# A recurrent attention layer and two MoE-shaped layers on one core: states in 64 columns, other start order, decay bounds in layer 2

## The chip, the core and the metric

The kernel runs on 1 core of one Trainium2 chip. The metric is the device time of one execution in microseconds (us). Most work is done by five engines that each run their own list of instructions in order: TensorE (PE in the profile; PEld is its loading of weights), VectorE (DVE), ScalarE (ACT), GpSimd (POOL) and SyncE (SP), which here only issues DMA transfers. Semaphores tie the lists together.

## The reference

The first part is a recurrent attention over 768 steps for 4 batches and 8 heads of 48 columns; its output goes through two feed-forward layers with 3072 tokens, 384 model columns and 2048 hidden ones.

```python
for t in range(S):
    cur = einsum('bhd,bhe->bhde', u[None] * kt, vt)
    y[:, :, t] = einsum('bhd,bhde->bhe', rt, state + cur)
    state = wt[:, :, :, None] * state + einsum('bhd,bhe->bhde', kt, vt)
x = y.transpose(0, 2, 1, 3).reshape(B * S, H * D)
h = x @ w_in;  x = (maximum(h, 0) + alpha * minimum(h, 0)) @ w_out      # layer 1
h = x @ w_in;  x = (h * clip(h + 3, 0, 6) / 6) @ w_out                  # layer 2
```

## The kernel before

**Attention.** The 768 steps are cut into thirds of 256 (12 in all, counted over the batches as t), and the 8 heads into 4 pairs. A unit n is one third of one pair; there are 48, and each third is two chunks (c) of 128 steps. The two heads of a pair lie on partitions 0 to 47 and 64 to 111. For a unit, L673 loads keys, reads and decays in one transfer; L691 and L705 are VectorE scans that give the products of decays to a chunk's end and their inverses; L726 scales keys and reads by them (`scale`); L781 multiplies scaled keys with reads for each head (48 rows, 128 columns, one PSUM bank per head); L789 transposes the keys, L820 copies them out; L827 and L831 make key-value products for the two heads; L876 or L878 brings the state Y to the next chunk. `state` (L853 on ScalarE, L855 on VectorE) scales Y into the tile sbd, a 112x112 matrix that is zero outside the two 48x48 diagonal blocks, with one instruction for each block. L764 puts the u terms on diagonals of X, L805 or L810 copies the triangle of L781's product over them. `pc` then sums the output y in PSUM: L907 multiplies sbd with the scaled reads (112 rows to 112 columns at once), L914 and L918 add X times v for the two heads (128 rows to 48 or 64 columns). Each fp32 product is two instructions in the trace. L702 (`keep`) keeps the smallest products of each unit for a check at the end.

**From attention to layer 1.** L943 and L949 split y into a high part and a rest (`hi_`, `lo_`), and write them into xt, the input of layer 1 for one block of 512 tokens (two thirds). Pairs 0 to 2 fill 112 of the 128 rows of their slab; the rows of pair 3 go to a tile x3, and six transfers per third (`spread`, L959) distribute 16 rows each to the free rows of the three slabs. They follow all eight outputs of the third.

**Layers.** A slot is one group of 128 hidden columns of one block: nine matmuls into h (L1176 to L1178: high by high, high by rest, rest by high, for three slabs), a gate on ScalarE and VectorE (L1214 and L1221, L1216 and L1225, L1231, L1234), and nine matmuls into three sums acc. There are 16 slots in a block, 6 blocks and 2 layers. The weights arrive packed; L128, L132, L135, L1140 and L1144 unpack them and split them likewise.

**Order.** Nothing of the order is left to a tool: class `Plan` collects all steps, each with the engines that may do it, an estimated duration for each, a due time and what it depends on. `run` then builds the lists greedily: the engine that can start earliest takes the step with the earliest due time. The tables URGENCY, GROUPS and SINGLE shift due times and fix engines. `issue` stands for SP, where a later transfer lands after an earlier one. Before the first slot, `keep_warm` fills gaps of TensorE with small matmuls (L1036), for the clock that is granted to it.

**Where.** Units 0 to 7 (`early`) feed block 0 and come before the first slot. Units 0 to 15 have TensorE steps of their own; later ones join the outputs of one unit with the key-value products of the next (`add_visit`) and the next unit's L781. In layer 2 the weights and the decays of units 24 to 47 are checked for range (`add_range`, `add_decay`), with slack.

Of the kernel before, what the change touches and what calls it, by code (L numbers as in the profile page):

```python
# [7 lines left out]
F32 = mybir.dt.float32  # L8
# [33 lines left out]
WARM = 400  # L42
SETTLE = 3
FUSE = 16
# [97 lines left out]
def weight_range(nc, v, raw):  # L142
# [8 lines left out]
    "add_drain.drain": {2: (-2.0, "DVE"), 3: (2.0, "ACT")},  # L151
    "add_drain.store": {2: (-6.75, None), 3: (-0.25, None)},
    "add_range.upper": {4: (2.5, None)},
    "add_slot.gate": {1: (-4.5, None), 2: (-3.0, None), 3: (-2.25, None)},
    "add_slot.ghi": {1: (-4.25, None), 2: (-5.0, None), 3: (-10.75, None)},
    "add_slot.glo": {1: (-1.5, "DVE"), 2: (3.75, None), 3: (-3.75, None)},
    "add_slot.h_": {1: (4.0, None), 2: (-4.0, None), 3: (-6.75, None), 4: (-1.0, None)},
    "add_slot.pq": {1: (-6.5, None), 2: (1.25, None), 3: (1.25, None)},
    "add_third.load_rk": {0: (1.25, None), 1: (-6.0, None), 2: (-2.25, None), 3: (-3.75, None)},
    "add_third.load_v": {0: (-4.5, None), 1: (-0.5, None), 2: (1.25, None), 3: (-5.75, None)},  # L160
    "add_third.red": {0: (-2.0, None), 1: (-4.25, None), 2: (7.0, None), 3: (-7.0, None)},
    "add_unit.add_output.hi_": {0: (-3.5, None), 1: (-6.75, None), 2: (3.25, None), 3: (-8.75, None)},
    "add_unit.add_output.lo_": {0: (-0.5, None), 1: (-2.75, None), 2: (-6.5, None), 3: (5.25, None)},
    "add_unit.add_states.newstate": {0: (-14.25, None), 1: (-4.5, None), 2: (-1.0, None), 3: (6.0, None)},
    "add_unit.check": {2: (-5.5, None), 3: (-7.25, None)},
    "add_unit.diag": {0: (-5.25, None), 1: (3.25, None), 2: (-5.25, None), 3: (-9.75, None)},
    "add_unit.keep": {0: (-0.25, None), 1: (4.75, None), 2: (-3.25, None), 3: (-18.0, None)},
    "add_unit.kt": {0: (-8.75, None), 1: (0.75, None), 2: (-6.5, None), 3: (-3.25, None)},
    "add_unit.kv": {0: (-4.5, None)},
    "add_unit.load": {0: (-3.25, None), 1: (-6.75, None), 2: (-5.75, None), 3: (3.75, None)},  # L170
    "add_unit.pa": {0: (-8.25, None), 1: (-2.75, None)},
    "add_unit.recip": {0: (-0.25, None), 1: (-3.25, None), 2: (8.5, None)},
    "add_unit.scan_g": {0: (-2.5, None), 1: (-5.5, None), 2: (-5.0, None), 3: (8.25, None)},
    "add_unit.scan_t": {0: (5.75, None), 1: (-9.75, None), 2: (6.75, None), 3: (-12.5, None)},
    "add_unit.triangle": {0: (-2.0, None), 1: (-4.0, None), 2: (2.25, None), 3: (-1.5, None)},
    "add_weights.hi": {0: (3.0, None), 1: (1.25, None)},
    "add_weights.lo": {0: (3.5, "POOL"), 1: (-2.25, None)},
    "add_weights.load": {0: (-3.75, None), 1: (-2.0, None)},
    "add_weights.rest": {0: (17.25, None), 1: (-1.75, None)},
    "join": {0: (-1.5, None), 1: (0.25, None)},  # L180
    "load_alpha": {0: (-5.75, None)},
    "load_u": {0: (-3.5, None)},
    "negate": {0: (-7.5, None)},
    "output": {0: (-4.5, None), 1: (-5.75, None)},
    "scale": {0: (0.5, None), 1: (-2.25, None), 2: (-0.5, None), 3: (-2.0, "DVE")},
    "scale_half": {0: (-5.0, "POOL")},
    "second": {1: (-2.25, None), 2: (-5.25, None), 3: (5.5, None), 4: (2.0, None)},
    "sign": {0: (3.0, None), 1: (5.25, None)},
# [153 lines left out]
class Plan:  # L342
# [165 lines left out]
    def keep_warm(self, seq):  # L508
# [3 lines left out]
        for o in seq:  # L512
            if o.get("filler"):
                continue
# [1106 lines left out]
```

## Time and profile before

| what | us |
|---|---|
| median of 3 runs | 928.58 |
| lowest and highest run | 927.21, 931.37 |
| the profiled execution | 926.92 |
| its span from the first to the last instruction | 925.1 |
| TensorE busy in the span | 912.8 |
| VectorE busy | 551.1 |
| ScalarE busy | 520.8 |
| GpSimd busy | 121.9 |

Busy time of TensorE counts from an instruction's start to its modelled end, and instructions overlap: a 512-column matmul is shown with 0.39 us, while the next one starts 0.23 us behind it. The step from start to start is what counts in a full string. An idle time stands in brackets with what ended it.

### The profile page before, as it was taken

How to read it: one execution, taken by the hardware profiler on the slowest of the kernel's cores; microseconds unless marked ns; L12 is line 12 of the kernel's file. 1: busy time of each engine (PE TensorE's matmuls, PEld its weight loads, DVE VectorE, ACT ScalarE, POOL GpSimd, SP SyncE). 2: the span in 40 equal slices, each digit the busy share in tenths (PEclk: the TensorE clock that was granted, in tenths of full speed). 3: DMA queues.
4: the chain of work that ended last, by engine and by line, in shares of the span. 5: the costliest groups of instructions: out<-in, count | busy, mean ns of one | idle time of the engine just before them, and what ended most of it. 6: DMA issues, size and time to landing. Idle time of an engine off the chain costs nothing.

```text
span 925.1 us, 13568 instructions
## 1 busy us (share of the span) xinstructions
PE 912.8 (99%) x4936; PEld 749.0 (81%) x4936; DVE 551.1 (60%) x1061; ACT 520.8 (56%) x1174; POOL 121.9 (13%) x109
## 2 busy tenths in 40 slices
PE   8889999999999999999999999999999999999998
PEld 6677788888888888888888888888888888888886
DVE  8989988667878655753347775343353443443432
ACT  5989974545545545453359997363363453553332
POOL 4410120011021231311022241000000000000000
PEclk9999999999999999999999999999999999999999
DMA  9888333222323302110136530060250330430001
GB/s 279 259 260 278 99 89 99 72 60 84 114 68 99 112 17 70 31 44 10 35 119 214 192 124 1 24 203 9 75 161 1 113 122 1 119 118 1 35 1 38
DMA packets 39628, 88.97 MB, mean 96 GB/s; under 512 B 5248, under 2 KB 10368, under 8 KB 39552
## 3 DMA queue, kind: packets, MB, share of 16 engines
q1 hardware_dynamic: 39120, 87.22, 30.7%
q8 instruction: 41, 0.67, 0.3%
q10 hardware_dynamic: 432, 0.79, 0.2%
q14 instruction: 35, 0.29, 0.1%
HBM read 76.19 MB, written 9.44 MB: 93 GB/s over the span
## 4 chain that ended last, share of the span: by engine, by line
PE 94%; DVE 3%; DMA 2%; SPq 0%; issue 0%; ACT 0%; DVEq 0%
PE h L1176 14%; PE acc L1176 14%; PE h L1177 14%; PE h L1178 14%; PE acc L1177 14%; PE acc L1178 14%; PE A L781 3%; PE y L914 2%; PE y L907 2%; PE A L789 1%; DMA wraw<-in_w 1%; DMA un<-in_unit 1%; PE y L918 0%; DVE tg L691 0%; DVE rk L635 0%
## 5 line engine op out<-in xcount | busy, mean ns | idle before, releaser
L1176 PE MATMUL acc<-g,w 128*128 128x512 f32 x576 | 226.6, 393 | 0.0
L1177 PE MATMUL acc<-g,w 128*128 128x512 f32 x576 | 224.3, 389 | 0.0
L1178 PE MATMUL acc<-g,w 128*128 128x512 f32 x576 | 224.3, 389 | 0.0
L1231 ACT ACTIVATE g<-pg 128x512 fp32r<-128x512 f32 x192 | 120.6, 628 | 126.3 <-PE acc L1178 106.5
L1234 DVE TENSOR_TENSOR g<-pg,g 128x512 fp32r<-128x512 f32 x141 | 99.9, 709 | 132.8 <-ACT g L1231 132.5
L1176 PEld LDWEIGHTS acc<-g,w 128*128 128x128 f32 x576 | 108.6, 189 | 22.7 <-issue 0.6
L1178 PEld LDWEIGHTS acc<-g,w 128*128 128x128 f32 x576 | 108.1, 188 | 22.6
L1177 PEld LDWEIGHTS acc<-g,w 128*128 128x128 f32 x576 | 108.2, 188 | 21.8 <-DVE g L1234 0.3
L1225 DVE SCALAR_TENSOR_TENSOR pg<-q,h 128x512 f32<-128x512 f32 x96 | 65.7, 685 | 95.2 <-ACT q L1216 95.0
L1234 POOL TENSOR_TENSOR g<-pg,g 128x512 fp32r<-128x512 f32 x51 | 73.6, 1444 | 363.6 <-ACT g L1231 250.6
L1216 ACT ACTIVATE q<-h,three 128x512 f32<-128x512 f32 x96 | 65.8, 685 | 92.6 <-PE h L1178 92.5
L1176 PE MATMUL h<-xt,w 128*128 128x512 f32 x288 | 115.0, 399 | 2.0 <-DMA xt<-x 2.0
L1178 PE MATMUL h<-xt,w 128*128 128x512 f32 x288 | 112.7, 391 | 0.0
L1177 PE MATMUL h<-xt,w 128*128 128x512 f32 x288 | 112.6, 391 | 0.0
L1176 PE MATMUL h<-x,w 128*128 128x512 f32 x288 | 112.0, 389 | 0.0
L1177 PE MATMUL h<-x,w 128*128 128x512 f32 x288 | 112.0, 389 | 0.0
L1178 PE MATMUL h<-x,w 128*128 128x512 f32 x288 | 112.0, 389 | 0.0
L1214 ACT ACTIVATE q<-h,nal 128x512 f32<-128x512 f32 x96 | 65.7, 685 | 82.2 <-PE h L1178 77.8
L1221 DVE SCALAR_TENSOR_TENSOR pg<-h,q 128x512 f32<-128x512 f32 x96 | 65.9, 686 | 40.0 <-ACT q L1214 25.2
L764 ACT ACTIVATE X<-ident,p 128x128 f32<-128x128 f32 x192 | 60.6, 390 | 11.7 <-PE y L918 11.3
L1176 PEld LDWEIGHTS h<-xt,w 128*128 128x128 f32 x288 | 54.8, 190 | 13.4 <-DMA xt<-x 2.1
L1178 PEld LDWEIGHTS h<-xt,w 128*128 128x128 f32 x288 | 54.3, 189 | 11.5
(102 smaller groups left out, 1222.4 us busy)
## 6 DMA issues: line engine op xcount, KB each, us to landing
wraw<-in_w SPq DMA_DIRECT2D x64, 384.0 KB, 5.6
un<-in_unit SPq DMA_DIRECT2D x48, 337.3 KB, 3.5
raw<-in_w SPq DMA_DIRECT2D x32, 384.0 KB, 3.3
rk<-in_tok SPq DMA_DIRECT2D x24, 384.0 KB, 3.8
v<-in_vch SPq DMA_DIRECT2D x12, 384.0 KB, 4.1
x2d<-st SPq DMA_DIRECT2D x18, 256.0 KB, 2.2
x2r<-x2d SPq DMA_DIRECT2D x18, 256.0 KB, 5.0
out<-st SPq DMA_DIRECT2D x15, 256.0 KB, 2.6
```

The lines of the kernel that those rows point to most:

```text
L764: nc.scalar.activation(X[:, i], ident, AF.Copy, scale=pp[:, i : i + 1])
L781: nc.tensor.matmul(A[h][:, cs], kr[r0 : r0 + D, 0, cs], kr[r0 : r0 + D, 1, cs], start=True, stop=True,)
L907: nc.tensor.matmul(y[:, cs], S[c], u["kr"][:, 1, cs], start=(c == inter[0]), stop=False, skip_group_check=True,)
L1176: nc.tensor.matmul(ps, whi, xhi, start=start, stop=False, skip_group_check=True)
L1177: nc.tensor.matmul(ps, whi, xlo, start=False, stop=False, skip_group_check=True)
L1178: nc.tensor.matmul(ps, wlo, xhi, start=False, stop=stop, skip_group_check=True)
L1214: nc.scalar.activation(q, k["h"], AF.Relu, scale=nal[:, f : f + 1])
L1216: nc.scalar.activation(q, k["h"], AF.Relu, bias=three)
L1221: nc.vector.scalar_tensor_tensor(out=p, in0=k["h"], scalar=0.0, in1=k["q"], op0=ALU.max, op1=ALU.subtract)
L1225: nc.vector.scalar_tensor_tensor(out=p, in0=k["q"], scalar=6.0, in1=k["h"], op0=ALU.min, op1=ALU.mult)
L1231: nc.scalar.activation(k["g"][:, 0], k["p"], AF.Copy)
L1234: eng[e].tensor_tensor(out=k["g"][:, 1], in0=k["p"], in1=k["g"][:, 0].bitcast(F32), op=ALU.subtract)
```

## The change

- `sbd` has 64 columns instead of 112, and both heads' states lie in its columns 0 to 47, on their own rows. `state` scales them in one instruction of 112x48. `pc` multiplies each head apart: rows 0 to 47 into y rows 0 to 63, rows 64 to 111 into y rows 64 to 111.
- The pairs of a third run in the order 3, 0, 1, 2. After each of pairs 0, 1 and 2, two transfers spread the rows of x3 that this pair's slab needs, with high part and rest in one. For units 3 and 7 (`SPLIT`) output is written in two row halves, and their transfers wait for pair 3 alone.
- Units 0 to 3 (`PARTED`) load their decays first and keys and reads in a second transfer.
- The outputs y of odd units below 8 use a bank of the pool of h.
- `keep` is done for units 24 to 47 only; for units 0 to 23 `add_decay` repeats the scan in layer 2 and copies the smallest products.
- The matmuls that fill TensorE before the first slot are no longer a fixed supply, and the rule for the gaps that they leave has changed. ScalarE instead of GpSimd fills `wa`.
- The planner has other constants, and the three tables other values (not shown).

```diff
-WARM = 400
+PARTED = 4
+SPLIT = (3, 7)
...
-    LOAD = 1.3
+    LOAD = 1.25
+    FIRST, RUSH, SLUGGISH = 2.7, 12.0, 1.2
...
-    COLD = 8.0
+    COLD = 0.0
...
-    SLACK, STARTED, STEADY = 0.5, 5.0, 15.0
-    BEGIN = {"PE": 1.5, "DVE": 4.0, "ACT": 6.0, "POOL": 4.0, "SP": 0.7}
+    SLACK, IDLE, SPAN, STARTED = 0.45, 0.7, 3.4, 5.0
+    BEGIN = {"PE": 1.5, "DVE": 2.8, "ACT": 4.3, "POOL": 2.6, "SP": 0.7}
...
+            if o["eng"] == "PE" and not began:
+                gap = o["start"] - t
+                idle = [(a, x) for a, x in idle if a > o["start"] - self.SPAN]
+                slack = max(0.0, min(self.SLACK, gap, self.IDLE - sum(x for a, x in idle)))
...
-    sbd = [const.tile([PR, PR], F32, name=f"sbd{i}") for i in range(4)]
+    sbd = [const.tile([PR, 64], F32, name=f"sbd{i}") for i in range(4)]
...
-            nc.gpsimd.memset(wa[i], 0)
+            nc.scalar.activation(wa[i], none.broadcast_to([P, 2 * DM]), AF.Copy)
...
-        t, pr = divmod(n, NPAIR)
+        t, pr = n // NPAIR, (n + 3) % NPAIR
...
-        o_load = plan.op({"SP": 0.95}, d - 4 if n else -50.0, load, new=[ub_])
+        at = d - 4 if n else -50.0
+        if n < PARTED:
+            o_load = plan.op(
+                {"SP": 0.35}, at - 0.2, lambda e: load(e, 2 * TH, UW), new=[ub_],
+                kind="add_unit.load",
+            )
+            o_in = plan.op(
+                {"SP": 0.63}, at, lambda e: load(e, 0, 2 * TH), new=[ub_], kind="load_kr"
+            )
+        else:
+            o_in = o_load = plan.op({"SP": 0.95}, at, load, new=[ub_])
...
-        plan.op({"ACT": 0.21}, d + 2, keep, [o_t], use=[tgb])
+        if n >= LATER:
+            plan.op({"ACT": 0.21}, d + 2, keep, [o_t], use=[tgb])
...
-            F = u["T"][:, c, 0:1]
-            for r0 in (0, 64):
-                rows, block = slice(r0, r0 + D), S[c][r0 : r0 + D, r0 : r0 + D]
-                if e == "ACT":
-                    nc.scalar.activation(block, Y()[rows, :], AF.Copy, scale=F[rows])
-                else:
-                    nc.vector.tensor_scalar(block, Y()[rows, :], F[rows], None, op0=ALU.mult)
+            F, block = u["T"][:, c, 0:1], S[c][:, 0:D]
+            if e == "ACT":
+                nc.scalar.activation(block, Y(), AF.Copy, scale=F)
+            else:
+                nc.vector.tensor_scalar(block, Y(), F, None, op0=ALU.mult)
...
         def room(e):
+            if alt:
+                return ps_h.tile([PR, 2, TH], F32, tag="h", name=f"y{n}")
             return ps_a.tile([PR, 2, TH], F32, tag="y", name=f"y{n}")
...
-                nc.tensor.matmul(
-                    y[:, cs], S[c], u["kr"][:, 1, cs], start=(c == inter[0]), stop=False,
-                    skip_group_check=True,
-                )
+                for r0, m in ((0, 64), (64, D)):
+                    nc.tensor.matmul(
+                        y[r0 : r0 + m, cs], S[c][r0 : r0 + D, 0:m], u["kr"][r0 : r0 + D, 1, cs],
+                        start=(c == inter[0]), stop=False, skip_group_check=True,
+                    )
...
+            rows = ((0, D), (64, PR)) if split else ((0, PR),)
...
             if pr == 3:
...
+                x3_ops[t] = [o_hi, o_lo]
+                return
...
+            def spread(e, h):
+                nc.sync.dma_start(
+                    XT[j][48 + 64 * h : 64 + 64 * h, pr, :, cs].bitcast(F32),
+                    X3[t][64 * h + 16 * pr : 64 * h + 16 * pr + 16].bitcast(F32),
+                )
+
+            before = x3_ops[t] + ([] if split else [o_hi, o_lo])
+            for h in range(2):
+                ops.append(
+                    plan.op(
+                        {"SP": 0.15}, d + 2.6 - (3.0 if split else 0.0),
+                        lambda e, h=h: spread(e, h), before, new=[xt_buf[j]], use=[x3b_[t]],
+                        kind="spread",
                     )
...
+        for c in range(2):
+            last = [
+                plan.op(
+                    {"DVE": 0.73}, due + 1 + c, lambda e, c=c: falls(e, c), [o] + last, new=[fb],
+                    use=[rb], pair=True, kind="decay_falls",
+                )
+            ]
+            last = [
+                plan.op(
+                    {"DVE": 0.15}, due + 1.5 + c, lambda e, c=c: lowest(e, c), last, use=[fb],
+                    kind="decay_lowest",
+                )
+            ]
```

`falls` is the scan of L691 on one unit's decays (112x258), `lowest` a copy of two values per partition into `fall`.

## Rows read from the trace of the kernel before

**Rows 1.** The page's part 1: busy us (share of the span) and count per engine.

```profile
PE 912.8 (99%) x4936; PEld 749.0 (81%) x4936; DVE 551.1 (60%) x1061; ACT 520.8 (56%) x1174; POOL 121.9 (13%) x109
```

**Rows 2.** Windows: length, PE, PEld, DVE, ACT, POOL busy; clock, DMA share, GB/s.

```profile
50.00:56.00 6.00, 5.25 (x17) 4.30 (x18) 3.81 (x9) 3.45 (x9) 1.09 (x1) 0.72 0.91 286
56.00:130.00 74.00, 74.00 (x452) 58.48 (x451) 69.61 (x131) 68.18 (x141) 10.35 (x9) 1.00 0.61 194
130.00:430.00 300.00, 300.00 (x1889) 248.47 (x1888) 206.73 (x451) 151.94 (x417) 52.77 (x39) 1.00 0.24 69
430.00:905.00 475.00, 475.00 (x2097) 393.15 (x2096) 221.92 (x354) 255.34 (x489) 37.51 (x26) 1.00 0.26 81
```

**Rows 3.** Waits of TensorE over the span: us in total, times, longest us.

```profile
PE A L827 <- ACT kT L820: 2.3, 5, 0.7
PE h L1176 <- DMA xt<-x: 2.0, 1, 2.0
```

**Rows 4.** SP's timeline from 43 us, and the chain that ended last (start, us).

```profile
44.01 4.45 SPq L959 DMA_DIRECT2D xt<-x  x6
...
47.87 2.77 DMA xt<-x
```

**Rows 5.** Timeline of TensorE, 50 to 59 us: start, us, instruction, idle time before.

```profile
50.75 0.77 PE L1176 MATMUL h<-xt,w 128*128 128x512 f32 x1 [2.01 <-DMA xt<-x]
...
56.09 0.39 PE L1178 MATMUL h<-xt,w 128*128 128x512 f32 x1
```

**Rows 6.** Timeline of VectorE, 0 to 54 us.

```profile
8.01 0.70 DVE L691 TENSOR_TENSOR_SCAN tg<-un,restart 112x258 f32<-112x258 f32 x1 [1.92 <-DMA un<-in_unit]
...
39.28 0.43 DVE L949 TENSOR_TENSOR xt<-y,xt 112x256 fp32r<-112x256 f32 x1
...
43.58 0.41 DVE L949 TENSOR_TENSOR x<-y,x 112x256 fp32r<-112x256 f32 x1
```

**Rows 7.** Groups of VectorE, 0 to 44 us: busy us, mean ns, idle before.

```profile
L705 DVE TENSOR_TENSOR_SCAN tg<-un,gfirst 112x258 f32<-112x258 f32 x10 | 7.5, 746 | 0.1
L691 DVE TENSOR_TENSOR_SCAN tg<-un,restart 112x258 f32<-112x258 f32 x10 | 6.7, 681 | 2.3 <-DMA un<-in_unit 2.3
...
L642 DVE TENSOR_REDUCE p<-rk 128x8 f32<-128x384 f32 x6 | 3.3, 544 | 0.1
L635 DVE TENSOR_TENSOR rk<-rk,u_sb 128x384 f32<-128x384 f32 x6 | 3.2, 538 | 0.0
...
L878 DVE SCALAR_TENSOR_TENSOR Y<-Y,tg,A 112x48 f32<-112x48 f32 x12 | 3.0, 252 | 0.0
...
L855 DVE TENSOR_SCALAR sbd<-Y,tg 48x48 f32<-48x48 f32 x6 | 2.6, 431 | 0.0
```

**Rows 8.** The tile x (x3 of the code), 0 to 60 us: its transfers.

```profile
DMA to landing us min/median/max: 2.0/3.4/5.8
```

**Rows 9.** Timeline of TensorE, 60.8 to 63 and 65.1 to 67.4 us.

```profile
61.37 0.72 PE L781 MATMUL A<-kr 48*128 48x128 f32 x8
...
65.37 0.39 PE L1178 MATMUL h<-xt,w 128*128 128x512 f32 x1
65.60 0.60 PE L907 MATMUL y<-kr,sbd 112*112 112x128 f32 x4
66.13 0.31 PE L914 MATMUL y<-X,v 128*48 128x128 f32 x1
66.14 0.31 PE L918 MATMUL y<-X,v 128*48 128x128 f32 x1
66.28 0.27 PE L914 MATMUL y<-X,v 128*48 128x128 f32 x1
```

**Rows 10.** Lines L781 (60 to 75 us) and L914 (65 to 67): min/median/max ns.

```profile
L781 PE MATMUL A<-kr x16: 272/272/373, 61.4 to 69.5; 48*128 48x128 f32 x16
...
L914 PE MATMUL y<-X,v x4: 272/273/310, 66.1 to 66.5; 128*48 128x128 f32 x4
```

**Rows 11.** Groups of TensorE, 56 to 430 us.

```profile
L907 PE MATMUL y<-kr,sbd 112*112 112x128 f32 x132 | 20.8, 272 | 0.0
```

More of the change, by code (lines that the diff above doesn't have):

```diff
@@ L176 @@
[L176 to L185, printed above, removed]
@@ new lines @@
+    "add_weights.hi": {0: (0.25, None), 1: (-2.25, None)},
+    "add_weights.lo": {0: (-6.75, None), 1: (-1.5, None)},
+    "add_weights.load": {1: (-2.5, None)},
+    "add_weights.rest": {0: (3.0, None), 1: (-2.0, None)},
+    "join": {0: (-7.25, None)},
+    "load_alpha": {0: (-2.0, None)},
+    "load_kr": {0: (2.0, None)},
+    "load_u": {0: (-1.0, None)},
+    "negate": {0: (-13.5, None)},
+    "output": {0: (5.25, None), 1: (3.0, None)},
+    "scale": {0: (1.0, "POOL"), 1: (-1.0, "POOL"), 2: (3.0, None), 3: (-3.0, None)},
@@ L416, in step @@
         else:
-            d = o["where"][e] * (2 if e == "PE" and t < self.COLD else 1)
+            d = o["where"][e]
             if e == "PE" and state["began"] and t - state["PE"] > self.LULL:
@@ L947, in lo_ @@
             def lo_(e):
                 hi, lo = parts()
-                nc.vector.tensor_tensor(out=lo, in0=u["y"], in1=hi.bitcast(F32), op=ALU.subtract)
-            fresh = [xt_buf[j]] + ([x3b] if x3b else [])
-            o_hi = plan.op({"ACT": 0.6}, d + 2.5, hi_, [o_pc], new=fresh, use=[yb2])
-            o_lo = plan.op({"DVE": 0.41}, d + 2.5, lo_, [o_hi], new=fresh, use=[yb2])
+                for a, b in rows:
+                    nc.vector.tensor_tensor(
+                        out=lo[a:b], in0=u["y"][a:b], in1=hi[a:b].bitcast(F32), op=ALU.subtract
+                    )
@@ L954, in add_output @@
+            fresh = [xt_buf[j]] + ([x3b_[t]] if pr == 3 else [])
+            more = len(rows)
+            o_hi = plan.op({"ACT": 0.06 + 0.46 * more}, d + 2.5, hi_, [o_pc], new=fresh, use=[yb2])
+            o_lo = plan.op({"DVE": 0.07 + 0.34 * more}, d + 2.5, lo_, [o_hi], new=fresh, use=[yb2])
             ops += [o_hi, o_lo]
             if pr == 3:
[L958 to L962 removed]
@@ L1026, in fast_path, with warm @@
     warm_t = {}
-    def add_warm(count):
-        plan.group = "warm"
-        wb = plan.buf("acc2", 1)
-        def warm(e):
-            if "ps" not in warm_t:
-                warm_t["ps"] = ps_acc.tile([P, 2 * P], F32, tag="acc2", name="warm")
-            some = ident.bitcast(BF16)
-            nc.tensor.matmul(warm_t["ps"], some[:, 0:P], some, start=True, stop=True)
-        for i in range(count):
-            plan.op({"PE": 0.27}, 1000.0, warm, new=[wb])["filler"] = True
+    def warm(e):
+        if "ps" not in warm_t:
+            warm_t["ps"] = ps_acc.tile([P, 2 * P], F32, tag="acc2", name="warm")
+        some = ident.bitcast(BF16)
+        nc.tensor.matmul(warm_t["ps"], some[:, 0:P], some, start=True, stop=True)
+    plan.warm = {
+        "fn": warm, "kind": "add_warm.warm", "filler": True, "id": -1, "due": 1000.0,
+        "group": "warm", "where": {"PE": 0.27}, "full": set(), "order": set(), "pair": False,
+    }
     def add_settle(due, after):
```

292 lines of the change are left out of this document (142 added, 150 removed), and 86 rows, old and new, of the table SINGLE.

## The prediction

> **What bounds the kernel now.** I read the page first: TensorE is busy 99% of the span [rows 1], so time can leave in three ways only: fewer or cheaper matmuls, less time before TensorE is fed without a break, or waits taken out. The table of windows tells which of them is open in which stretch [rows 2]. From 56 to 130 us TensorE is full, but VectorE (69.6 of 74 us) and ScalarE (68.2) are nearly full too. From 130 to 430 us, the rest of layer 1, only TensorE is full; from 430 us on (layer 2) VectorE is below half. The table of TensorE's waits confirms it: the two longest sums are 2.3 us for kT, in five pieces, and 2.0 us in one piece for a transfer into xt before the first slot, which starts at 50.75 us [rows 3, 5]. So the kernel is a start of 50.75 us followed by an unbroken string of matmuls up to 920 us. The change can win in the start, and whatever it adds to TensorE's string it pays in full.
>
> **Where the start ends.** The last output of units 0 to 7 leaves VectorE at 43.58 + 0.41 = 43.99 us [rows 6]. Then SP issues six spread transfers from 44.01 us on, 4.45 us of issuing, and the last of them lands 2.77 us after its issue at 47.87 us [rows 4]. The first slot starts at 50.75 us. Its 18 matmuls reach to 56.09 + 0.23 us, 5.57 us, where 18 steps of the usual 0.227 us (65.60 less 65.37 [rows 9]) are 4.08 us. These 1.5 us are the clock: it was granted at 0.72 of full speed on average in 50 to 56 us, after 2.01 us in which TensorE stood idle [rows 2, 5]. The mean lies between the two levels of 1.2 and 2.4 GHz: the string was entered at the lower one.
>
> **The tail of the start.** After the change the pair of the third that supplies the spread rows comes first, each later pair spreads its own 16 rows by two transfers, and for units 3 and 7 these wait only for the third's first pair. So none of the six issues lies behind unit 7. What is left behind it is its own output, now in two halves: one more VectorE instruction of 0.41 us [rows 6] and one more on ScalarE that I put at as much, together 0.8 us. The gain is 50.75 - 43.99 - 0.8 = 5.9 us. It is smaller if unit 6's two transfers land late: they are issued some 39.28 + 0.43 + 0.6 = 40.3 us, and a spread took 2.0 to 5.8 us to land [rows 6, 8]. At worst 46.1 us, a gain of 4.6 us.
>
> **The start itself.** VectorE works through 10 to 44 us almost without a gap, so work that leaves it, or is put off, counts. Up to 44 us it holds [rows 7]: of six 48x48 state instructions (2.6 us in all) three of 112x48 remain, 0.25 each as L878 takes for that shape, 1.8 us saved; work for units 8 and 9 that the first slot doesn't need, two of the ten L691 (0.68 each), one L705 (0.75), four L635 (0.54) and two L642 (0.54), 5.3 us; and the 1.92 us of idle time before unit 1's scan at 8.01 us, which waited for a load [rows 6] and now needs only that load's last third, with some 0.3 us before unit 0's. Together 9.3 us if the new order uses all of it and nothing else becomes late, 0 if the chain through GpSimd, TensorE and ScalarE, which also took its turns here, is what counts. No row decides between the ends, so I take half, 4.7 us. The first slot then starts at 50.75 - 5.9 - 4.7, some 40.1 us (35.5 to 46.1).
>
> ScalarE loses the L702 copies and the second state instructions, and gets two fills of wa before its first real work; GpSimd loses these fills. Splitting the first four unit loads costs SP four more issues, 0.74 us each by L959's rate (4.45 us for six [rows 4], the dearest at hand), that stand ahead of later loads: 0 as long as VectorE has other work, at most 3.0 us, which the lower end of that gain includes.
>
> **Work that falls back into the string.** TensorE did units 8 and 9 in part while it waited for the first slot. With the slot 10.6 us earlier, about one unit (2.0 us in the string) is still to be done after it; 0 to 3.1 us.
>
> **The clock.** The new padding bounds the idle time before the first slot and the wait for the transfer is gone: -1.5 us (0 at worst).
>
> **What is added to TensorE.** Each L907 product of 112 rows and 112 columns becomes two of 48 rows, one into columns 0 to 63 and one into 64 to 111. The count of L907 doubles. Whether this costs streaming time is read from the neighbours: L914 and L918 start in pairs 0.01 us apart (66.13 and 66.14), next pair 0.15 later, and the eight 48-row L781 take 0.72 us from the first's start to the last's end [rows 9], where eight in sequence at L907's step of 0.11 (0.60 less 0.27, by three) would need 7 x 0.11 + 0.27 = 1.04. So row halves and column halves both run two at a time, and I take the eight quarter products as four steps of 0.109 us, as before: 0.
>
> But the array changes its division, and that shows. L907 follows a 512-column matmul at the usual step (65.37 to 65.60): no cost. L907's fourth starts at 65.60 + 0.60 - 0.27 = 65.93; the next could start at 66.04, but L914 starts at 66.13 [rows 9], and its first takes 310 ns where 273 is the median; the first L781 takes 373 instead of 272 [rows 10]. So a change of division costs 0.09 us of drain and 0.04 (48 columns) to 0.10 us (128 columns) of weight load that nothing covers. Today a visit pays it between L907 and L914; afterwards it pays once before L907 and again behind it. One more per visit, with 64 columns: 0.14 us (0.13 to 0.19). 132 L907 lie in 56 to 430 us [rows 11], 27 visits with four and 12 with two; with the unit that falls back it is 40 visits: +5.6 us (5.2 to 7.6). Nothing covers this, since TensorE is full there.
>
> **Can the others follow?** With all this, block 0 ends 10.6 + 1.5 - 2.0 - 8 x 0.14 = 9.0 us earlier, so VectorE and ScalarE must deliver earlier by as much. VectorE has 4.4 us idle in 56 to 130 and 2.2 in 50 to 56 us [rows 2]; halved state instructions of units 8 to 15 give 1.5 more. It is short by some 1 us, unless GpSimd, used 10.4 of 74 us, takes more of the scaling. ScalarE has 5.8 + 2.6 us idle, and loses half of its state instructions and the L702 copies of units up to 23: enough. I put down +1.0 us (0 to 4.6, what is missing if only the idle time of 56 to 130 us is used).
>
> **The 24 decay bounds in layer 2** add 24 scans (0.68 each) and 24 small copies to VectorE, some 20 us, in the idle 253 of 475 us [rows 2]. Each can hold a gate back by 0.7 us; TensorE has a second h and a third g to use meanwhile. Cost 0; if that cover were gone, up to 17 us. New orders in layer 2 and later blocks move no wait that costs today: 0.
>
> **The sum**: -10.6 - 1.5 + 2.0 + 5.6 + 1.0 = -3.5 us. The profiled execution took 926.92 us (its span 925.1 and 1.8 around it), so 923.4; the median of the runs shown is 1.66 us higher, and on that scale it is 928.58 - 3.5 = 925.1 us.
>
> **Rivals.**
> (1) *The quarter products don't overlap.* Both write one bank of PSUM; L781's two halves, which do overlap, write two banks, and L914 with L918, which share one, differ in columns only. No row shows two row halves in one bank. In sequence they add 27 x 4 x 0.109 + 12 x 2 x 0.109 = 14.4 us: 939.5 us, slower. It makes the kernel slower by over 0.5% from 8.1 us on, that is once more than half of the pairs run in sequence. The Trainium skill, "TensorEngine Tiling (Array Packing)", Restrictions and Gotchas (Gotcha 1), says that different row tiles cannot access the same PSUM bank simultaneously; by that rule this rival would be the forecast. Against it stands the trace: the two halves here differ in columns as well, and column halves do share a bank at 0.01 us distance. Chance 0.11.
> (2) *VectorE takes over as the bound* in 50 to 130 us: the 9.0 us of earlier delivery come back as waits of TensorE for g, w and X. Then -3.5 - 1.0 + 9.0 = +4.5: 933.1 us. For it: 69.6 of 74 us. Against it: GpSimd's idle time. Chance 0.14.
> (3) *The change of division costs nothing net*, because the drain before L907 replaces the one behind it: -9.1 us, 919.5 us. For it: a visit's later change from L831 to L781 isn't visible as a separate gap in the rows. Against it: L914's and L781's first instructions. The Trainium skill (same page, Key Properties) says that changing the tiling mode drains TensorE; by that rule there are two drains, as in the forecast. Chance 0.17.
> (4) *The start gives all it can*: first slot at 35.5 us (4.6 us more), one more us of units falls back: -7.1 us, 921.5 us. Chance 0.16.
> If the transfers still end the start (46.1 us, hardly any work falling back), the sum is about +0.5 us; that lies in the forecast's own range of 921.5 to 930, chance 0.42.
>
> **How the numbers follow.** A measurement of this kernel tells 0.5%, 4.6 us, from no change: faster is below 923.9, slower above 933.2 us. Faster: rivals 3 and 4 nearly whole (0.15 + 0.15) and the lower end of the forecast (0.10): 0.40. Slower: rival 1 (0.11), half of rival 2 (0.06) and a rest (0.01): 0.18. Same: 0.42. The range of 918 to 935 us leaves out rival 1 above and some 0.07 at the lower end.
>
> **What would show it.** The first slot's L1176 near 40 us without a wait for xt, its 18 matmuls at 0.227 us; six L959 per third issued in twos; L907 x8 in pairs, with the string between neighbouring 512-column matmuls longer by 0.14 us per visit; TensorE's waits after the first slot of about 1 us; no wait in layer 2. I am wrong if L907 starts singly, if the first slot stays above 46 us, or if TensorE shows waits of several us between 40 and 130 us.

## The result: slower by 0.7%, and the profile after

| | before | after |
|---|---|---|
| median, us (lowest to highest) | 927.4 (926.96 to 931.37) | 935.15 (931.14 to 936.9) |
| ratio to before, 95% interval | 1 | 1.0068 [1.0044, 1.0092] |
| the profiled execution, us | 926.92 | 931.72 |
| its span | 925.1 | 929.9 |
| start of the first slot | 50.75 | 43.34 |
| from there to the start of the last slot matmul | 869.01 | 879.79 |
| from there to the end of the span | 5.38 | 6.81 |

The forecast was 925.1 us, faster by 0.4%. The same kernel timed again came to 1.0076 [1.006, 1.0093]. The table's last three lines make up the difference of the spans: -7.4 + 10.8 + 1.4 = +4.8 us. The start gained most of what was forecast; the string of matmuls behind it lost more than that.

The page's part 1 of the kernel after, which answers to [rows 1]:

```profile
PE 919.1 (99%) x5105; PEld 742.8 (80%) x5105; DVE 542.9 (58%) x1019; ACT 512.4 (55%) x1150; POOL 141.8 (15%) x126
```

Its windows (length; busy time of PE, PEld, DVE, ACT, POOL; granted clock, DMA share, GB/s), which answer to [rows 2]:

```profile
43.00:50.00 7.00, 5.89 (x32) 4.23 (x31) 6.92 (x16) 5.96 (x14) 1.09 (x1) 1.00 0.95 305
50.00:56.00 6.00, 4.82 (x49) 3.54 (x49) 5.86 (x13) 5.47 (x15) 1.32 (x1) 1.00 1.03 336
56.00:60.00 4.00, 4.00 (x22) 2.91 (x21) 4.00 (x8) 4.00 (x10) 0.00 (x0) 0.57 1.05 313
56.00:130.00 74.00, 74.00 (x454) 56.50 (x453) 65.75 (x118) 64.33 (x125) 10.32 (x9) 0.98 0.53 171
130.00:430.00 300.00, 300.00 (x1958) 240.84 (x1959) 184.12 (x379) 145.39 (x408) 57.29 (x47) 1.00 0.24 71
430.00:905.00 475.00, 475.00 (x2126) 392.18 (x2123) 239.93 (x392) 256.69 (x499) 58.11 (x41) 1.00 0.26 82
```

TensorE is full from 56 us on, as before, but the 13 us behind the start of the first slot hold 2.3 us of idle time, and the clock then runs at 0.57 for 4 us: the four microseconds lose 4 x (1 - 0.57) = 1.7 us of work. VectorE and ScalarE got lighter in 56 to 130 us (65.8 and 64.3 of 74 us, where they had 69.6 and 68.2 [rows 2]), and yet TensorE waits.

TensorE's waits of the kernel after, which answer to [rows 3]:

```profile
PE A L729 <- DVE X L758: 1.7, 2, 1.2
PE h L1163 <- DVE pg L1208: 1.1, 1, 1.1
```

Its timeline of TensorE from 42 us (start, us, instruction, idle time before), which answers to [rows 5]:

```profile
42.62 0.72 PE L729 MATMUL A<-kr 48*128 48x128 f32 x8
43.34 0.47 PE L1163 MATMUL h<-xt,w 128*128 128x512 f32 x1
...
49.29 0.50 PE L1163 MATMUL h<-xt,w 128*128 128x512 f32 x1 [1.11 <-DVE pg L1208]
...
51.56 0.71 PE L729 MATMUL A<-kr 48*128 48x128 f32 x8
52.45 0.65 PE L856 MATMUL y<-kr,sbd 48*64 48x128 f32 x8
...
54.95 0.71 PE L729 MATMUL A<-kr 48*128 48x128 f32 x8 [1.18 <-DVE X L758]
55.84 0.95 PE L856 MATMUL y<-kr,sbd 48*64 48x128 f32 x8
...
57.74 0.80 PE L1163 MATMUL h<-xt,w 128*128 128x512 f32 x1
```

The wait for xt is gone from the table. In its place stand a wait for a gate of VectorE (1.11 us) and one for a triangle (1.18 us). The first of them stands in VectorE's list. Timeline of ScalarE and VectorE:

```profile
45.77 0.69 ACT L1201 ACTIVATE q<-h,nal 128x512 f32<-128x512 f32 x1 [0.76 <-PE h L1165]
...
48.55 0.68 DVE L1208 SCALAR_TENSOR_TENSOR pg<-h,q 128x512 f32<-128x512 f32 x1
```

The gate's input from ScalarE is ready at 46.46 us; VectorE, busy almost without a break, has four other steps ahead of it and takes it at 48.55 us. Between 51.56 and 57.74 us two visits to units follow one another with no slot matmul between them: when the second visit's L729 waits, TensorE's list holds nothing else. Before, twelve slot matmuls stood between the first two visits behind the first slot. From 55.84 to 59.46 us the instructions are longer: eight L856 take 0.95 us instead of 0.65, a slot matmul 0.80 instead of 0.4 to 0.5. For most of these 4 us the clock is at the lower of its two levels, 1.2 GHz.

### The profile page after: what moved, and what is told of

It is laid out like the page before. It is cut to its first block, busy times and chain, and to the rows that moved or that the text cites. A ratio compares the mean times of both kernels' runs of the same rounds, so it can differ in the third digit from the quotient of the medians.

```text
span 929.9 us, 13918 instructions
## 1 busy us (share of the span) xinstructions
PE 919.1 (99%) x5105; PEld 742.8 (80%) x5105; DVE 542.9 (58%) x1019; ACT 512.4 (55%) x1150; POOL 141.8 (15%) x126
## 4 chain that ended last, share of the span: by engine, by line
PE 94%; DMA 2%; DVE 2%; ACT 0%; issue 0%; SPq 0%; DVEq 0%; ACTq 0%
PE acc L1163 14%; PE acc L1165 14%; PE h L1163 14%; PE acc L1164 14%; PE h L1165 14%; PE h L1164 14%; PE A L729 3%; PE y L856 2%; PE y L863 2%; PE A L737 1%; DMA wraw<-in_w 1%; DMA rk<-in_tok 1%; DMA un<-in_unit 1%; DVE rk L571 1%; PE y L867 0%
## 5 line engine op out<-in xcount | busy, mean ns | idle before, releaser
L1212 DVE SCALAR_TENSOR_TENSOR pg<-q,h 128x512 f32<-128x512 f32 x96 | 65.8, 686 | 94.2 <-ACT q L1203 93.8
L1221 POOL TENSOR_TENSOR g<-pg,g 128x512 fp32r<-128x512 f32 x48 | 68.4, 1426 | 303.1 <-ACT g L1218 301.5
L674 POOL TENSOR_TENSOR kr<-un,tg 112x512 f32<-112x512 f32 (+1 forms) x39 | 41.1, 1055 | 229.0 <-DVE tg L652 139.5
```

The costliest lines, as they stand in the source:

```text
L674: eng[e].tensor_tensor(out=u["kr"][:, i].rearrange("p a (c s) -> p a c s", c=2), in0=u["in"][:, 0 : 2 * TH].rearrange("p (a c s) -> p a c ...
L1212: nc.vector.scalar_tensor_tensor(out=p, in0=k["q"], scalar=6.0, in1=k["h"], op0=ALU.min, op1=ALU.mult)
L1221: eng[e].tensor_tensor(out=k["g"][:, 1], in0=k["p"], in1=k["g"][:, 0].bitcast(F32), op=ALU.subtract)
```

## The experiments

Theory 1: the string lost time in two places, by one more change of the array's division at each visit, and by waits and a falling clock behind the earlier first slot. Rival A: the quarter products run one after the other. Rival B: VectorE has become the bound in 43 to 60 us. Rival C: the transfers have. All ratios are to the kernel before.

**The two kernels once more, unchanged.**

> The changed kernel once more, unaltered. Its seven runs lie in two groups, 931.1 to 931.7 and 934.2 to 936.9 us, and the profiled one (931.72) is of the lower group. If waits of TensorE between 43 and 60 us, and the lower clock behind them, differ from execution to execution, this profile shows another sum of them than 2.3 us of waits and one stretch at 0.57, and its time moves by the same amount. If the groups come from the end (landing of the last stores, 1.4 us longer in the profiled one than before), the string from first to last matmul is the same 879.8 us again and the end differs.

> The kernel before, unaltered, for a second profile. In the profiles of the changed kernel and of three variants, 6.8 to 7.6 us lie between the start of the last matmul and the end; in the one profile of before it is 5.4. If that end depends on the kernel, it is 5.4 again; if it is the landing of the last store on this chip, it is about 7.3, and 2 us of the 4.8 between the two profiled spans are nothing that the change made. The ratio should be 1.000.

Measured: 1.0076 [1.006, 1.0093] and 0.9995 [0.9978, 1.0013]. The profile of the kernel before starts its first slot at 52.02 us this time (50.75 before); its string lasts 867.66 us, 1.35 less, since the clock is at 1.00 in 50 to 56 us where [rows 2] have 0.72. The kernel after again has two waits (0.81 and 1.62 us, the second for kr of GpSimd this time), its string lasts 881.34 us, 1.55 more than in its first profile, and its clock falls to 0.50 in 56 to 60 us, as its windows show:

```profile
56.00:60.00 4.00, 4.00 (x21) 2.83 (x18) 3.98 (x8) 3.70 (x10) 0.00 (x0) 0.50 1.04 293
60.00:64.00 4.00, 4.00 (x17) 2.80 (x16) 1.62 (x4) 2.24 (x6) 1.09 (x1) 0.74 1.04 393
```

**One part alone: states in 64 columns and quarter products, in the kernel before.**

```diff
-    sbd = [const.tile([PR, PR], F32, name=f"sbd{i}") for i in range(4)]
+    sbd = [const.tile([PR, 64], F32, name=f"sbd{i}") for i in range(4)]
...
-                nc.tensor.matmul(
-                    y[:, cs], S[c], u["kr"][:, 1, cs], start=(c == inter[0]), stop=False,
...
+                for r0, m in ((0, 64), (64, D)):
+                    nc.tensor.matmul(
+                        y[r0 : r0 + m, cs], S[c][r0 : r0 + D, 0:m], u["kr"][r0 : r0 + D, 1, cs],
```

> The kernel before with one part of the change alone: states in 64 columns, one state instruction, the product of states and reads in two halves of 48 rows. Planner and order are those of before. Theory A (each visit pays one more change of the array's division, 0.136 us measured in the changed kernel): 39 visits behind the first slot, +5.3 us in the string, first slot up to 1.5 us earlier from fewer state instructions: +4 to +5.3 us, ratio 1.004 to 1.006. Rival B (the division change is paid only where the string was about to wait anyhow): 0 to -1.5 us.

Measured: 1.0064 [1.0043, 1.0084]. The string lasts 872.78 us, 3.8 more than in the profile of before; without the slow clock of 50 to 56 us that profile would be 1.5 us shorter, so 5.3 us. No wait of TensorE stands in the string. This part alone costs about as much as the whole change. The first slot starts at 48.80 us, 2.0 and 3.2 us sooner than in the two profiles of before, and the last slot matmul 1.8 and 1.9 us later, where the ratio stands for 5.9 us: the profiled execution was the fastest of its eight (930.94 us, of up to 937.91).

**One part undone: 112-column states in the kernel after** (the reverse of that diff).

> The changed kernel with that one part undone: states as 112x112 blocks, two state instructions, one product of 112 rows; planner, estimates and order as in the changed kernel. Theory A: 40 visits x 0.136 = 5.4 us less in the string; up to 1.5 us later start because VectorE and ScalarE have more state instructions: 4 to 5.4 us faster than the changed kernel, about level with before (ratio 0.999 to 1.002). Rival C (what costs are the waits of TensorE and the lower clock between 43 and 60 us): more state instructions make these waits longer, the time stays at the changed kernel's (ratio 1.005 and over).

Measured: 1.0031 [1.0013, 1.0048]; the string lasts 875.85 us, 3.9 less than after, with 1.9 us more of waits and the clock at 1.00; the first slot comes 1.2 us later (44.53 us). The same visit in both, first of the kernel after, then of this one (timeline of TensorE):

```profile
68.44 0.40 PE L1165 MATMUL acc<-g,w 128*128 128x512 f32 x1
68.77 0.65 PE L856 MATMUL y<-kr,sbd 48*64 48x128 f32 x8
69.35 0.31 PE L863 MATMUL y<-X,v 128*48 128x128 f32 x1
...
69.92 0.50 PE L1163 MATMUL h<-xt,w 128*128 128x512 f32 x1
```

```profile
68.51 0.40 PE L1166 MATMUL acc<-g,w 128*128 128x512 f32 x1
68.74 0.60 PE L857 MATMUL y<-kr,sbd 112*112 112x128 f32 x4
69.28 0.31 PE L864 MATMUL y<-X,v 128*48 128x128 f32 x1
...
69.85 0.50 PE L1164 MATMUL h<-xt,w 128*128 128x512 f32 x1
```

From slot matmul to slot matmul the visit takes 69.92 - 68.44 = 1.48 us with quarter products and 1.34 without. (The three most frequent kinds of visit, counted in the same way, went from 2.16, 2.16 and 2.37 us before to 2.30, 2.29 and 2.51 after.) Of the extra 0.14 us, 0.10 lies ahead of the products: L856 starts 0.33 us behind the slot matmul, L857 the usual 0.23. The rest lies between their start and that of L863 or L864, 0.58 us against 0.54. Eight L856 take 0.65 us, where eight in sequence would take 7 x 0.11 + 0.29 = 1.06. They run two at a time, into one bank: rival A is out.

**Rival B: less work for VectorE.** In the kernel after, the second products (L571) of thirds 2 and 3 are left out.

```diff
-                    {"POOL": 1.03, "DVE": 0.55}, due + 2 + c, lambda e, b=b, m=mul: m(e, b=b),
+                    {"POOL": 1.03, "DVE": 0.55}, due + 2 + c,
+                    lambda e, b=b, m=mul: None if t in (2, 3) else m(e, b=b),
```

> The changed kernel without the eight products of reads, keys and u of thirds 2 and 3 (L571 for t = 2 and 3 left out, so the diagonal terms of units 8 to 15 are not the reference's); everything else in its place and order. This takes some 4.4 us off VectorE and GpSimd between 25 and 75 us. Rival C (VectorE is the bound between 43 and 60 us, its lateness makes TensorE wait 2.3 us and brings the lower clock): the waits and the stretch at 0.57 go, 3 to 5 us faster than the changed kernel, ratio 1.002 to 1.004 against before. Theory A alone (only the string is longer): the first slot may come up to 2 us earlier, the rest stays, ratio 1.005 to 1.008.

Measured: 1.0075 [1.0054, 1.0096], first slot at 43.85 us, 2.3 us of idle time in the first 16 us of the string. In 43 to 50 us VectorE is busy 4.73 of 7 us, and TensorE waits as long as before: the wait for the gate is down to 0.25 us, the one for the triangle stays at 1.18, and 0.8 us of waits for kT and for a load of weights are new. What VectorE has to do in sum isn't the bound.

**Rival C: less to transfer.** The token loads of thirds 2 and 3 go too, 1.57 MB, with all their products and reductions; and the same in the kernel before, as a control.

```diff
+                if t in (2, 3):
+                    return
...
+                if t in (2, 3):
+                    p_t[t] = p_t[t - 2]
+                    return
```

> The kernel after without the token loads, their products and the reductions that make the token factors of thirds 2 and 3 (the factors of thirds 0 and 1 stand in their place); about 1.57 MB less is moved early on. Theory that the transfers feed the stretch behind the first slot (in the kernel after the DMA engines are 95 to 105% busy in 43 to 60 us): the weights of units 7 to 9 land 2 to 5 us earlier, TensorE's two waits behind the first slot (1.1 and 1.2 us) shrink to under 0.5 us in sum, the first slot starts at 39 to 42 us instead of 43.3, and the ratio to the kernel before falls from 1.007 to 1.000 to 1.004. Rival, that VectorE's and ScalarE's order of work feeds it and the transfers do not: the waits stay at 1.5 to 2.5 us and the ratio at 1.006 to 1.009, as in the run without the products.

> The kernel before with the same token loads, products and reductions of thirds 2 and 3 left out (the control). If the earlier landing is worth something only where the first slot is due early: ratio 0.998 to 1.001, with a first slot at 49 to 51 us. If the transfers delay the start of either kernel alike: first slot 3 to 5 us earlier and ratio 0.995 to 0.997.

Measured: 1.0068 [1.005, 1.0086], and 0.9989 [0.9977, 1.0002] for the control. The first slot starts at 42.12 us (51.10 in the control), the first wait is gone (VectorE takes the gate 0.11 us after ScalarE has its input ready), 0.39 us for kT and the second wait (1.19 us) are there, and the clock falls again. The queue fills with later loads: the DMA engines are still 98 to 105% busy in 50 to 60 us. So the run doesn't show what lighter transfers would bring, and rival C stays open. But it shows what the second wait is made of. Two windows of this kernel:

```profile
50.00:56.00 6.00, 4.43 (x45) 3.07 (x41) 5.13 (x9) 6.00 (x15) 1.09 (x1) 0.77 1.05 314
56.00:60.00 4.00, 4.00 (x13) 2.82 (x9) 2.22 (x5) 2.76 (x9) 1.09 (x1) 0.50 0.98 350
```

The timeline of all its engines, 51 to 53 us:

```profile
51.10 0.25 ACT L775 ACTIVATE kT<-A 128x112 f32<-128x112 f32 x1
...
51.40 0.26 PE L782 MATMUL A<-v,kT 128*64 128x48 f32 x1 [0.39 <-ACT kT L775]
...
51.85 0.26 DVE L831 SCALAR_TENSOR_TENSOR Y<-Y,tg,A 112x48 f32<-112x48 f32 x1 [0.58 <-PE A L786]
52.03 0.72 DVE L765 COPY_PREDICATED X<-mask,A 128x512 f32<-128x512 uint8 x1
...
52.90 0.38 PE L736 MATMUL A<-kr 48*128 48x128 f32 x2 [1.19 <-DVE X L765]
```

The products with kT end at 51.71 us; VectorE, idle for 0.58 us, takes the running sum Y at once (51.85) and then the triangle (52.03 to 52.75), and only then is buffer A free for the next unit (52.90): 1.19 us. In the kernel after, where VectorE was busy up to Y, the same links take 1.18 us (53.76 to 54.95). So the second wait is the length of a chain and not VectorE's queue. TensorE waits it out, since its list has two visits side by side.

**The waits filled.** 8 and 10 small matmuls on a scratch tile go into TensorE's list at the two waits of the kernel after.

```diff
+            if o["eng"] == "PE" and began:
+                seen[o["kind"]] = seen.get(o["kind"], 0) + 1
+                for kind, nth, fill in (("add_slot.h_", 3, 8), ("add_unit.pa", 2, 10)):
+                    if o["kind"] == kind and seen[kind] == nth:
+                        kept += [dict(self.warm, eng="PE", start=t, end=t)] * fill
```

> The changed kernel with eight idle-time matmuls (bf16, 256 columns, 0.11 us each) before the first matmul of the third slot, where TensorE waited 0.8 to 1.1 us, and ten before the second unit product behind the first slot, where it waited 1.2 to 1.6 us. Theory D (the two waits bring TensorE to 1.2 GHz near 57 to 61 us, which costs 2 to 3 us on top of the waits): the windows behind show full clock, 2 to 3 us faster than the changed kernel, ratio 1.004 to 1.006. If the clock costs nothing because other engines hold TensorE up anyway: no change, 1.007.

Measured: 1.0026 [1.0009, 1.0044], against 1.0068 and 1.0076 without it. Windows of this kernel:

```profile
50.00:56.00 6.00, 6.00 (x61) 4.44 (x61) 5.73 (x12) 5.20 (x15) 1.32 (x1) 1.00 1.03 326
56.00:60.00 4.00, 4.00 (x30) 2.80 (x27) 4.00 (x8) 4.00 (x10) 0.00 (x0) 1.00 0.98 340
```

The filling does no work of the kernel, and 0.0042 to 0.0050, some 4 us, come back. In the windows the clock stays at 1.00. The profiles account for part of it, 1.7 us lost in 56 to 60 us in the kernel after and 6 x 0.06 + 4 x 0.50 + 4 x 0.26 = 3.4 us in 50 to 64 us of the one timed again. The timed executions say the same, since the record has the mean granted clock of each: 0.999 to 1.000 in all twelve of the filled kernel (1 less the clock, times the span, is 0.6 us on average), 0.995 to 1.000 in those of the kernel after (2.3 us, and 3.4 timed again). These means also hold the stretch behind the last matmul, where a lower clock costs nothing: up to 1.3 us of them in the profiles. The profile of the kernel without the second products, at 1.00, was its exception: its six executions lost 4.4 us on average (0.991 to 0.999). That the filling is worth some 4 us is shown, and that some 2 to 3 us of it can be the clock; what the rest is, is not.

**The control, and both parts mended.** 14 small matmuls ahead of the first slot in the kernel before; the kernel after with 112-column states and the filling (8 and 14).

```diff
+            if o["eng"] == "PE" and o.get("starts") and not slots:
+                kept += [spare.pop() for _ in range(14)]
+            slots += o.get("starts", False)
```

> The kernel before with fourteen more of the small matmuls ahead of the first slot, in the 2.0 us in which TensorE waits for the last spread transfers. In one of its two profiles the clock was 0.56 to 0.59 in 50 to 54 us, in the other full. If the clock falls there in most executions, 1 to 1.5 us faster (ratio 0.9985 to 0.999); if seldom, no change.

> The changed kernel with both remedies: states as 112x112 blocks (no further change of the division) and small matmuls in the two waits behind the first slot. The two single effects were 0.0042 (state blocks) and 0.0045 (fill) of the time of before. If they add, ratio 0.998 to 0.999, faster than both kernels; if the clock fell only because the quarter products work TensorE less than the full one (the profile with full blocks showed waits of 1.0 and 2.0 us at full clock), the fill adds nothing: 1.003.

Measured: 1.0004 [0.9989, 1.002] and 1.0019 [1.0003, 1.0035]. In the kernel before, filling that one wait wins nothing: its timed executions lose as much to the clock with it (2.9 us on average) as without (3.2 us). In the kernel after, undoing the states (worth 0.0037 alone) and filling (0.0042 alone) give 0.0007 together over the filling alone. The intervals are 0.0016 to 0.0018 to either side, so this is hardly the sum. The profiles show part of why: undoing the states saves 3.2 us of the filled kernel's string (878.66 to 875.48 us) and lets it start 1.25 us later (44.07 instead of 42.82 us). The rest isn't settled. No variant beat the kernel before.

**The first slot sooner.** The unpacking of a weight tile (L129), which waits for a transfer, goes behind unit 7's copy in ScalarE's list.

```diff
+        seq.insert(hi, seq.pop(rest))
```

> The changed kernel with one step moved in ScalarE's list: the unpacking of a weight tile (L129), which waits for its load until 40.9 us, goes behind unit 7's output copy instead of ahead of it. The first slot should start 1.0 to 1.3 us earlier. Theory E (what is won at the start is given back, because VectorE and ScalarE deliver the gates in their own fixed order): waits between the first and the third slot grow by the same amount, the time changes by less than 0.5 us. Rival F (the start is what counts): 1.0 to 1.3 us faster than the changed kernel.

Measured: 1.0071 [1.0044, 1.0098]. VectorE has unit 7's output 1.1 us sooner, and the first slot comes no sooner. Timeline of this kernel:

```profile
41.81 0.86 DVE L904 TENSOR_TENSOR xt<-y,xt 48x256 fp32r<-48x256 f32 x2 [0.15 <-ACT xt L897]
...
42.66 0.71 PE L729 MATMUL A<-kr 48*128 48x128 f32 x8
43.39 0.48 PE L1163 MATMUL h<-xt,w 128*128 128x512 f32 x1
```

Unit 8's L729 stands ahead of the slot in TensorE's list and starts at 42.66 us here as in the kernel after (42.62): it waits for GpSimd's kr. That was a second condition, due at the same time. Behind the first slot the string shows what becomes of the 1.1 us: VectorE takes the first gate at 47.45 instead of 48.55 us, the wait of 1.11 us is gone, and then TensorE waits 0.71 us for kT and 1.83 us for kr of GpSimd, 2.54 us instead of 2.29 in all. The waits that theory E expected between the first and the third slot came after it.

**The spreads late again.** All six spreads of the third wait for unit 7's output in the kernel after, as before the change.

```diff
+            if t == 1 and pr == 2:
+                for o in mine:
+                    o["full"] |= {o_hi["id"], o_lo["id"]}
```

> The changed kernel, but all six transfers that spread the rows of the second third wait for unit 7's output, as in the kernel before (estimates and tables unchanged; the planner's lists shift with it). First slot later by 3 to 6 us. Rival F (the start is what counts): 3 to 6 us slower than the changed kernel less about 2 us of unit work that TensorE then does before the slot: ratio 1.008 to 1.012. Theory E: the waits behind the first slot vanish, ratio 1.005 to 1.008, as the changed kernel.

Measured: 1.0085 [1.0063, 1.0107]. The first slot starts at 48.80 us, 5.5 us later than after, and the kernel is 0.0009 to 0.0017 slower, 0.8 to 1.6 us. By these medians the sooner first slot, on which most of the forecast's gain rested, is worth 15 to 30% of its length; each ratio has some 2 us to either side, so it can be anything from nothing up to 4.6 us. From profile to profile the last slot matmul starts 3.3 us later (926.45 us against 923.13), 60%. It isn't worth its whole length in either reading. What it loses is seen in the string: 877.65 us with no wait before 218 us, 0.8 us behind it and the clock at 1.00, where the kernel after has 879.79.

**The order and the spreads alone, in the kernel before**, with its states and due times.

```diff
+SPLIT = (3, 7)
...
-        t, pr = divmod(n, NPAIR)
+        t, pr = n // NPAIR, (n + 3) % NPAIR
```

> The kernel before with another part alone: pair 3 of a third first, two transfers after each later pair, for units 3 and 7 ahead of their output, which is written in two row halves. Due times of all other steps, estimates and tables are those of before (the transfers have no entry of their own in SINGLE). First slot 5 to 7 us earlier than 52.0 us. Theory E (what is won at the start is mostly given back): some 2 to 4 us of unit work falls behind the first slot, waits of 1 to 3 us appear before 60 us, time within 1.5 us of before. Rival F (the start is what counts): 3 us faster or more, ratio below 0.997.

Measured: 1.0068 [1.0044, 1.0092], though the first slot starts at 46.84 us, 3.9 sooner than in the first profile of before and 5.2 sooner than in the second. Windows:

```profile
88.00:92.00 4.00, 2.24 (x29) 1.52 (x27) 4.00 (x7) 4.00 (x11) 0.00 (x0) 0.99 0.98 278
92.00:96.00 4.00, 4.00 (x15) 2.88 (x14) 4.00 (x10) 3.96 (x8) 0.00 (x0) 0.59 0.06 20
```

The string lasts 876.99 us, 8.0 more than in the first profile of before: 2.6 us of waits (the longest 1.4, for kT), 2.0 for one visit more, 1.6 for the clock in 92 to 96 us less the 1.5 that before lost itself, and some 1.1 for twelve more changes of division (141 against 129, at the 0.09 us of the forecast). 2.2 us of it stay unexplained. The tables of due times here are those made for the old order; whether the new order would cost less with tables of its own wasn't tried in this kernel. The two parts don't add: each alone costs about as much as the whole change (1.0064 and 1.0068). That the same falling clock turns up 30 us later, in another order of work, speaks against a cause in one instruction of the new order.

## Why the prediction was wrong, point by point

| term of the sum, us | predicted | measured (profile to profile) |
|---|---|---|
| first slot sooner | -10.6 | -7.4 |
| clock | -1.5 | +0.2 (1.7 lost in 56 to 60, 1.5 no longer lost at 50.8) |
| one more unit in the string | +2.0 | +2.0 |
| one more change of division per visit | +5.6 | +5.4 |
| TensorE's waits behind the first slot | +1.0 | +2.3 |
| other changes of division | 0 | +0.9 (the rest of the string; up to eight changes more than before besides the forty) |
| behind the last slot matmul | 0 | +1.4 |
| sum | -3.5 | +4.8 |

Two steps failed: the size of the start itself (3.2 us), and the clock with the waits (3.0 us together). The lines with 0 (2.3 us) had no term at all.

**The start itself: the largest miss of the sum, 3.2 us.** The tail of the start went as forecast. The spreads are out of the way: no wait for xt is left, and those of a third are issued in twos, or four in a row, the last of them at 40.9 us:

```profile
L919 SPq DMA_DIRECT2D xt<-x x12: 585/592/739, 17.0 to 40.9; - x12
```

The forecast put unit 7's output at about 40 us; VectorE took the first half of it at 42.91 us. A piece of the kernel after's chain that ended last, and then its timeline:

```profile
32.24 8.57 DMA wraw<-in_w
```

```profile
40.84 1.72 POOL L674 TENSOR_TENSOR kr<-un,tg 112x512 f32<-112x512 f32 x1 [1.74 <-DVE tg L652]
40.89 1.08 ACT L129 ACTIVATE wa<-wraw 128x768 uint16<-128x768 uint32 x1 [0.19 <-DMA wraw<-in_w]
...
41.83 0.36 ACT L897 ACTIVATE xt<-y 48x256 fp32r<-48x256 f32 x1
...
42.91 0.42 DVE L904 TENSOR_TENSOR xt<-y,xt 48x256 fp32r<-48x256 f32 x1 [1.31 <-ACT xt L897]
```

A load of weights took 8.57 us to land, the unpacking that waits for it (L129) stands ahead of unit 7's copy in ScalarE's list, and VectorE is idle for 1.31 us. In the kernel before the same unpacking (L128) came behind that copy:

```profile
42.44 0.36 ACT L943 ACTIVATE x<-y 112x256 fp32r<-112x256 f32 x1
...
43.97 1.05 ACT L128 ACTIVATE wa<-wraw 128x768 uint16<-128x768 uint32 x1
```

The forecast had no term for what the new order puts ahead of unit 7 in ScalarE's list. (The two fills of `wa` that it did name run from 2.02 to 3.59 us, and ScalarE is idle for 3.35 us behind them: they cost nothing.) With that mended, GpSimd's kr for unit 8 (done at 42.56 us) was just as late. So if the tail gave its 5.9 us, 1.5 are left of the 4.7 that I had taken as half of 9.3 for the start itself, the term that no row decided.

**The quarter products: right, and with them the fall of rival 1.** In pairs, 40 visits, 0.14 us each. The groups of L856, 43 to 930 us, which answer to [rows 11]:

```profile
L856 PE MATMUL y<-kr,sbd 48*64 48x128 f32 x136 | 23.6, 287 | 0.0
L856 PE MATMUL y<-kr,sbd 48*48 48x128 f32 x136 | 23.0, 283 | 0.0
```

272 in 28 visits of eight and 12 of four: one visit more than before. The Trainium skill, "TensorEngine Tiling (Array Packing)", Restrictions and Gotchas (Gotcha 1), has different row tiles unable to access one PSUM bank at the same time; here the measurement decides: two quarters that differ in rows and in columns did so, eight in 0.65 us. Key Properties on the same page of the Trainium skill, by which a change of tiling mode drains TensorE, agree with the 0.14 us. Rival 3, by which the extra change costs nothing, is out by the same rows.

**The clock and the waits: the step that failed.** I counted the clock's loss at 50.75 us as won, and asked of the others only whether they have enough idle time in sum. They had: VectorE is less busy than before in 56 to 130 us. But what TensorE waits for behind the first slot is the order in VectorE's list and then a chain (kT on ScalarE, its products, Y and the triangle on VectorE; kr on GpSimd in the kernel timed again), and TensorE's list no longer had slot matmuls to lay over it. The waits came to 2.3 us where I had put 1.0, and with them the loss by the clock came back 5 us behind the place where it had been: +0.2 us where I had put -1.5. The timed executions show no clock won either: over a whole execution they lose on average 2.8 to 3.3 us in the kernel before, and 2.3 and 3.4 in the kernel after. The two terms together missed by 3.0 us, and filling the waits gave some 4 us back. Rival 2 had the place nearly right (50 to 130 us; the waits end at 49.3 and 55.0) and the cause in part: the first wait is VectorE's list, the second stays when VectorE has less to do. Its time, 933.1 us, lies near the measured one by luck, since it has 9.0 us of waits and 2.3 were measured.

**The range.** 918 to 935 left out 935.15 by 0.15 us, far less than the executions differ (931.14 to 936.9). The terms' upper ends together reach -4.6 + 0 + 3.1 + 7.6 + 4.6 = +10.7 us, 939.3 us; the range is narrower, and names only rival 1 as left out above. Of the terms with an upper end only the clock's went beyond it, +0.2 us where I had 0 at worst: that a new wait could bring the clock down again wasn't in the sum.

**The 1.4 us behind the last slot matmul can't be put down to the change.** The last step of the chain in the profiles of before, before again, after and after again:

```profile
920.15 1.94 PE settle L1049 x6
```

```profile
920.07 1.94 PE settle L1049 x6
```

```profile
923.53 1.94 PE settle L1005 x6
```

```profile
924.61 1.94 PE settle L1005 x6
```

Their spans end at 925.1, 927.3, 929.9 and 931.6 us: 5.0, 7.3, 6.4 and 7.0 us later. The two profiles of the kernel before differ by more than the two kernels do, and the kernel after with the late spreads has 5.0 us again.

**Right at no cost:** the decay bounds in layer 2. VectorE is busy 239.9 of 475 us there instead of 221.9 [rows 2], and no wait of TensorE's table lies behind 430 us.

**Still open.** The timed executions of the kernel after lie up to 5 us above its profiled one (931.72, of 931.14 to 936.9), those of the filled one on both sides of its own (930.88, of 929.48 to 933.36). The strings end 3.4 and 4.5 us later in the two profiles of after than in those of before, where the ratio stands for 6.3 us. The clock doesn't explain that: by the record the executions of the kernel after lose 2.3 us to it on average, the profiled one 1.8, and timed again 3.4, the profiled one 4.7. The 2.2 us of the order alone and why neither the two parts of the change nor the two mended parts add are open too.

## What to carry to other kernels

Starting a saturated engine sooner pays only as far as the list behind the start is fed sooner too: look at what lies between two dependent visits in that list, not at the idle sums of the engines that feed it. Count every change of the array's division, since in a full TensorE string it is paid in full (0.14 us here, forty times). Where a short wait of TensorE can't be removed, fill it with small matmuls and time that: here it gave back some 4 us for 2.3 us of waits.

## What the hardware showed unexpectedly

Behind the waits of the first 16 us of the string the clock fell in some kernels and not in others: to 0.57 (1.11 and 1.18 us idle), 0.50 (0.81 and 1.62), 0.50 (0.39 and 1.19) and 0.60 (0.71 and 1.83). It did not fall in the profile of the kernel without the second products (2.3 us in four pieces), nor in the one with 112-column states, whose waits of 1.02 and 1.95 us were longer; the window that holds the end of the second:

```profile
56.00:60.00 4.00, 3.33 (x27) 2.68 (x28) 3.95 (x7) 3.94 (x9) 0.61 (x1) 1.00 1.04 312
```

So the length of the waits alone doesn't decide it. Nor does the list of instructions: the mean granted clock over a whole execution of the six without the second products lies between 0.991 and 0.999, that of the nine with 112-column states between 0.996 and 1.000. Leaving out 1.57 MB of early loads left the DMA engines as busy in 50 to 60 us, at 98 to 105%, since later loads took the place.
